# A chunk attention and phase mixer: half of the phase weight on GpSimd's load queue, the first q and k in head halves

## The chip, the cores and the metric

The kernel runs on one core of one Trainium2 chip. The metric is the device time of one execution in microseconds (us). The engines of the core are TensorE (PE; its weight loads are shown as PEld), VectorE (DVE), ScalarE (ACT), GpSimd (POOL) and SyncE (SP); 16 DMA engines move data between HBM and on-chip memory. Engines run their own instruction streams in order and wait for each other through semaphores.

## The reference

Two stages, all inputs fp32. q, k and v are (8 batches, 8 heads, 576 tokens, 64). The first stage is attention inside chunks of 64 tokens; the second, with d_model = 512, mixes phases, tokens and channels.

```python
scores = scale * q_c @ k_c.T            # per batch, head and chunk of 64
attn = exp(scores - max) / sum
x = concat_heads(attn @ v_c)            # (8, 576, 512)

theta = x @ w_theta                     # phase weight, 512 x 512
zr, zi = x * cos(theta), x * sin(theta)
y = w_tok_r @ zr + w_tok_i @ zi         # along tokens, 576 x 576
u = x + y
out = u + max(u @ w_ch, 0)              # 512 x 512
```

## The kernel before

**Tiles.** Batches go in four pairs, p = 0 to 3. The 2 x 576 tokens of a pair are nine tiles of 128, in five groups: A and B are two tiles each of the pair's first batch, C and D two each of its second, and M is the middle tile, which has the last 64 tokens of both batches. A step is named by what it does, an optional part, the pair and the group: `L1.0A` is part 1 of step L for pair 0, group A. Part 0 and part 1 of an attention step are heads 0 to 3 and heads 4 to 7; of a later step they are the two tiles.

**The steps of a group.** `q`, `k`, `v` load it; `L`, `N` or `T` (`qk_t`, L276) transpose q and k on TensorE into PSUM; `tq` and `tkA`/`tkV` (L319) copy them out on VectorE or ScalarE; `S` is the score product (L358), `e` the exponential on ScalarE (L368, L374), `V` the product with v (L392), `n` the division (L404, L406). `X` or `Q` transposes x, `xA`/`xV` copies it (L453), `H` is x @ w_theta (`project`, L470), `g` the cosine and sine on ScalarE (L484, L488), `z` their products with x (L500 to L508). `Y` mixes the tokens (L542, L556), `y` adds x (L582), `U` or `R` transposes u, `W` is u @ w_ch (L470), `w` the ReLU and sum (L590), `s`/`sA` the store. `lw` loads a block of token weights (L227) and `TW` transposes it (L258). `D.n.b` are n products of a zero tile into bank b, which keep TensorE busy and have no other use (L269). `pe` and `pg` switch ScalarE's function table (L137).

**The order** is written out by hand: `ORDER` (L16) is a list of steps, walked once (L661), so every engine's instructions stand in the order of that list. The last numbers of a step are the PSUM banks it uses (8 banks; two steps that use one bank wait for each other's readers).

**Queues.** All loads that cast fp32 to fp16 on the way are issued by POOL: q and k (L180, L188, L193), v (L207, L217), token weights (L227) and w_ch (L243). The program gives POOL's loads eight completion semaphores in turn, and a load waits until the one eight before it has landed. `gate` (L164) also makes the loads of later pairs wait for a division of earlier work. The phase weight is different: `lt` (L229) has SP load it as two fp32 halves of 512 KB into tiles of the pool that q and k use too, and ScalarE (`ct0`) and VectorE (`ct1`) cast them (L240).

**The start.** POOL loads q.0B, builds the identity that the transposes need (`make_identity`, called in `init`, L131), and loads k.0B, then 0M, 0A and the v of 0B, 0A and 0M. TensorE runs 24 dummies, transposes 0B and 0M, runs 7 more dummies, and goes on with 0A.

Of the kernel before, what the change touches and what calls it, by code (L numbers as in the profile page):

```python
# [24 lines left out]
z0.0A z1.0A YA.0A.2 v.0D qP.1B kP.1B L.0D.0.1 tq.1A tkA.0D S.1A.4 V0.0C.6 y.0A e.1A q.1C tq.0D
YA.0B.2 n0.0C V1.0C.0 n1.0C V0.1A.4 V1.1A.6 n1.1A n0.1A YB.0B.2 lw.04 lc.00 q.1M X.0C.0 xV.0C
YM.0B.2 y.0B S.0D.6 Q.1A.4 xV.1A H.0C.0 e.0D V1.0D.2 n1.0D pg.00 g.0C V0.0D.6 H.1A.4 R.0B.2
n0.0D Q.0D.6 xV.0D g.1A k.1M q.1D TW.04.0 k.1D z.0C U.0A.1 H.0D.6 N.1B.4.5 uA.0B uV.0A tq.1B
g.0D z.0D tkA.1B k.1C W.0A.2 v.1C YC.0D.6 v.1B w.0A v.1D N.1M.1 tkV.1M T.1D.4 v.1M S.1B.2 pe.00
e.1B tq.1D tkA.1D tq.1M z.1A YM.0D.6 qP.2A sA.0A YD.0D.6 S.1M.2 twA.04 e.1M L.1C.5.4 tq.1C  # L30
Y.0M.0 y.0D tkA.1C S.1D.2 V1.1B.4 e.1D W.0B.6 V0.1D.2 kP.2A n1.1B S.1C.4 e.1C y.0M w.0B v.2A
YD.0C.0 q.2C q.2B k.2B n0.1D V0.1M.7 V0.1B.2 V1.1D.4 n0.1M V1.1M.6 YC.0C.0 n1.1M X.1M.6 n0.1B
n1.1D xA.1M U.0D.7 YM.0C.0 X.1B.2 v.3M y.0C sA.0B xV.1B q.2M k.2M X.1D.6 v.3D uA.0D N.2A.5.4
tkA.2A U.0C.7 xA.1D W.0D.0 tq.2A v.2B S.2A.2 e.2A R.0M.4 uV.0C uA.0M W.0C.6 V1.1C.2 V0.1C.4 w.0D
w.0C v.2M H.1M.0 pg.00 g.1M n1.1C n0.1C qP.2D W.0M.1 w.0M H.1B.6 V0.2A.4 Q.1C.0 q.3B H.1D.2 g.1B
n0.2A g.1D xV.1C v.3C H.1C.0 k.2C V1.2A.6 z.1M g.1C q.3C T.2B.4 k.3B z.1B tq.2B Y.1A.2 n1.2A
z.1D z.1C y.1A Q.2A.6 tkA.2B S.2B.0 v.2D Y.1D.4 pe.00 e.2B xA.2A V1.2B.6 y.1D V0.2B.0 n0.2B
n1.2B Y.1C.2 X.2B.0 T.2C.4 xV.2B T.2M.6 tq.2C Y.1B.0 tkV.2M tkA.2C S.2C.4 tq.2M S.2M.6 e.2C s.0D
y.1C k.3C kP.2D e.2M q.3A H.2A.2 g.2A y.1B R.1B.0 V0.2M.7 uV.1B v.3A v.2C V1.2M.6 n1.2M N.2D.4.5
n0.2M H.2B.0 g.2B X.2M.6 tkV.2D U.1A.5 v.3B uA.1A xV.2M tq.2D W.1B.2 H.2M.0 g.2M V1.2C.6 z.2A  # L40
# [6 lines left out]
R.2B.4 Q.3D.6 uA.1M e.3M xV.3D uA.2B W.1M.0 S.3C.2 V0.3A.6 y.2M w.1M H.3D.4 e.3C pg.00 g.3D
V1.3A.0 n0.3A n1.3A V1.3C.6 n1.3C W.2B.2 V0.3M.0 V1.3M.1 n1.3M n0.3M Q.3A.6 Y.2D.4 xV.3A R.2A.0
uA.2A w.2B V0.3C.6 y.2D H.3A.2 g.3A R.2C.0 n0.3C Q.3C.6 xV.3C W.2A.4 uV.2C z.3A X.3M.0 s.1C w.2A
H.3C.6 z.3D xA.3M H.3M.0 sA.1M g.3M z.3M W.2C.4 Y.3B.0 g.3C z.3C Y0.3D.2 w.2C y.3B R.2M.0 sA.2B  # L50
R.2D.6 s.2A R.3B.4 Y.3M.3 uA.2D W.2D.6 y.3M U.3M.3 uA.3B Y1.3D.4 y0.3D w.2D y1.3D W.3B.6 w.3B
s.2C s.3B uA.2M W.2M.0 w.2M uA.3M sA.2D Y.3A.2 y.3A Y1.3C.0 R.3A.6 uV.3A R1.3D.2 y1.3C s.2M
# [7 lines left out]
def kernel(  # L60
# [103 lines left out]
    def gate(p):  # L164

        if p and marks:
            nc.gpsimd.tensor_copy(out=seen, in_=marks.pop())
            marks.clear()

    def load_qk(p, g, which, plain):  # L170
        j0, bb, s0 = GROUPS[g]
# [12 lines left out]
        if plain:
            t = t.rearrange("p (j h d) -> p j h d", j=2, h=H)
            for j in range(2):
                t0 = s0 + j * P
# [39 lines left out]
            nc.gpsimd.dma_start(t[0:rows, ri], ap[i * P : i * P + rows, :])  # L227
# [382 lines left out]
    work = {  # L610
        "q": lambda p, g: load_qk(p, g, 0, False),
        "k": lambda p, g: load_qk(p, g, 1, False),
        "qP": lambda p, g: load_qk(p, g, 0, True),
        "kP": lambda p, g: load_qk(p, g, 1, True),
        "v": load_v,
        "lt": lambda p, g: load_theta(),
        "ct0": lambda p, g: cast_theta(0),
        "ct1": lambda p, g: cast_theta(1),
        "lc": lambda p, g: load_w_ch(),
        "lw": lambda p, i: load_tok(i),  # L620
        "init": lambda p, g: setup(),
        "pe": lambda p, g: table(AF.Exp),
        "pg": lambda p, g: table(AF.Sin),
# [80 lines left out]
```

## Time and profile before

| what | value |
|---|---|
| device time, median of 3 runs | 209.05 us (208.4 to 209.28) |
| the profiled execution | 206.72 us, of which its span 205.0 us |
| granted TensorE clock, mean of the span | 0.989 |
| busy: PE | 194.5 us (95%), 3467 products |
| busy: DVE, ACT, POOL | 130.2, 108.3, 94.7 us |
| q0, POOL's queue | 87568 packets, 16.01 MB |
| q1, SP's queue | 3472 packets, 6.42 MB |

The span runs from the first to the last instruction, and what lies around it, 1.72 us here, is start and end of the program. A busy share is an average over stages with different limits: the DMA engines are busy all through the first half and hardly in the last quarter, so the table alone does not say what bounds which stage. A load's time in the DMA view goes from its issue to the landing of its last part; with several loads in flight it is mostly time behind other loads.

### The profile page before, as it was taken

To read this page: it belongs to the slowest core of one execution; us is meant where nothing else is said; L and a number is where in the kernel's file an instruction comes from. 1 tells how busy PE (TensorE), PEld (TensorE's weight loads), DVE (VectorE), ACT (ScalarE), POOL (GpSimd) and SP (SyncE) were. 2 spreads that over 40 slices of the span, in tenths; PEclk is the share of its full clock that TensorE was granted. 3 is DMA by queue.
4 is the path that set the end of the run, shared out by engine and by line. 5 is a ranking of instruction groups with operands and counts; after the bars stand their busy time and mean duration, and the time that the engine had idled before them with its cause. 6 is when DMAs were issued, how large, how long until landed. Compare 5 with 4: busy or idle time off the path is not lost.

```text
span 205.0 us, 7674 instructions
## 1 busy us (share of the span) xinstructions
PE 194.5 (95%) x3467; PEld 103.6 (51%) x3467; DVE 130.2 (64%) x232; ACT 108.3 (53%) x133; POOL 94.7 (46%) x139
## 2 busy tenths in 40 slices
PE   7878999899969999999999999999999999999992
PEld 2355665556536575445546455555554544544441
DVE  0035875597655877893665888379767598253662
ACT  4044989339845168693038961489875345410211
POOL 7788894896977885986593460100000000000000
PEclk9979999999999999999999999999999999999998
DMA  6999999999999999999999995722020034224054
GB/s 211 157 166 126 176 188 170 123 137 163 164 176 191 117 204 222 217 148 161 79 160 82 130 152 36 102 106 106 3 106 3 3 92 168 106 101 155 3 184 176
DMA packets 93312, 26.99 MB, mean 132 GB/s; under 512 B 86368, under 2 KB 88288, under 8 KB 93280
## 3 DMA queue, kind: packets, MB, share of 16 engines
q0 software_dynamic: 87568, 16.01, 97.3%
q1 hardware_dynamic: 3472, 6.42, 8.8%
q10 hardware_dynamic: 2240, 4.06, 5.8%
q8 instruction: 27, 0.44, 0.9%
q14 instruction: 5, 0.04, 0.1%
HBM read 33.06 MB, written 9.44 MB: 207 GB/s over the span
## 4 chain that ended last, share of the span: by engine, by line
PE 78%; DMA 15%; POOL 3%; issue 2%; DVE 0%; ACT 0%; POOLq 0%; ACTq 0%; DVEq 0%
PE ps L556 29%; PE ps L470 29%; DMA v<-in_v_dram 8%; DMA qk<-in_q_dram 7%; PE ps L542 4%; PE ps L439 3%; PE ps L392 3%; PE ps L430 3%; PE ps L358 2%; PE ps L310 2%; PE ps L293 2%; POOL qk L193 1%; POOL wnat L227 1%; POOL v L217 1%; PE ps L297 0%
## 5 line engine op out<-in xcount | busy, mean ns | idle before, releaser
L556 PE MATMUL ps<-zi,wT 128*128 128x512 f16 x144 | 42.7, 379 | 1.8 <-issue 1.8
L556 PEld LDWEIGHTS <-wT 128*128 128x128 f16 x288 | 26.8, 98 | 32.4 <-issue 2.1
L556 PE MATMUL ps<-zr,wT 128*128 128x512 f16 x144 | 42.1, 380 | 0.0
L217 POOL DMA_DIRECT2D v<-in_v_dram x48 | 36.3, 777 | 10.2 <-DMA qk<-in_q_dram 3.7
L582 DVE TENSOR_TENSOR x<-ps,x 128x1024 f16<-128x1024 f32 (+1 forms) x22 | 22.5, 1026 | 22.6 <-PE ps L556 18.2
L470 PE MATMUL ps<-wch,uT 128*128 128x512 f16 (+1 forms) x148 | 34.3, 374 | 0.7 <-ACT uT L453 0.7
L470 PE MATMUL ps<-wtheta,xT 128*128 128x512 f16 x144 | 34.3, 380 | 0.0
L590 DVE SCALAR_TENSOR_TENSOR o<-ps,x 128x1024 f32<-128x1024 f32 (+2 forms) x23 | 22.6, 988 | 8.4 <-PE ps L470 6.5
L453 ACT COPY uT<-ps 128x1024 f16<-128x1024 f16 (+1 forms) x16 | 12.6, 800 | 28.8 <-PE ps L439 24.8
L374 ACT ACTIVATE eT<-ps 128x1024 f16<-128x1024 f32 (+1 forms) x18 | 16.6, 929 | 18.8 <-PE ps L358 18.8
L330 ACT COPY kT<-ps 128x1024 f16<-128x1024 f16 (+1 forms) x15 | 13.3, 901 | 24.9 <-DVE qT L326 13.4
L406 DVE TENSOR_TENSOR x<-ps,recip 128x512 f16<-128x512 f32 (+1 forms) x40 | 25.5, 638 | 1.4
L484 ACT ACTIVATE cos<-ps,pihalf 128x1024 f16<-128x1024 f32 (+1 forms) x22 | 21.1, 957 | 7.0 <-PE ps L470 6.7
L326 DVE COPY qT<-ps 128x1024 f16<-128x1024 f16 (+2 forms) x23 | 12.9, 570 | 17.5 <-PE ps L297 13.0
L470 PEld LDWEIGHTS <-uT 128*128 128x128 f16 x148 | 13.3, 98 | 15.1 <-ACT uT L453 1.9
L470 PEld LDWEIGHTS <-xT 128*128 128x128 f16 x144 | 12.9, 98 | 13.5
L488 ACT ACTIVATE sin<-ps 128x1024 f16<-128x1024 f32 (+1 forms) x22 | 19.0, 863 | 0.0
L193 POOL DMA_DIRECT2D qk<-in_q_dram x13 | 11.9, 920 | 1.4 <-POOLq L688 0.8
L404 DVE RECIPROCAL recip<-ps 128x8 f32<-128x8 f32 (+1 forms) x40 | 7.8, 195 | 7.4 <-PE ps L392 7.3
L453 DVE COPY xT<-ps 128x1024 f16<-128x1024 f16 (+1 forms) x13 | 8.1, 624 | 6.7 <-PE ps L439 4.0
L269 PE MATMUL ps<-zeros 128*128 128x512 f16 x33 | 11.0, 501 | 1.3 <-DVE pihalf L130 1.2
L193 POOL DMA_DIRECT2D qk<-in_k_dram x13 | 11.8, 913 | 0.7 <-issue 0.6
(59 smaller groups left out, 232.1 us busy)
## 6 DMA issues: line engine op xcount, KB each, us to landing
out_dram<-o SPq DMA_DIRECT2D x8, 512.0 KB, 3.4
qk<-in_q_dram POOLq DMA_DIRECT2D x13, 256.0 KB, 6.1
qk<-in_k_dram POOLq DMA_DIRECT2D x13, 256.0 KB, 7.0
out_dram<-o ACTq DMA_DIRECT2D x6, 512.0 KB, 4.1
v<-in_v_dram POOLq DMA_DIRECT2D x40, 64.0 KB, 5.8
v<-in_v_dram POOLq DMA_DIRECT2D x16, 128.0 KB, 6.1
wraw<-in_moe_w_theta_dram SPq DMA_DIRECT2D x2, 512.0 KB, 3.8
qk<-in_q_dram POOLq DMA_DIRECT2D x6, 128.0 KB, 4.9
```

The costliest lines, as they stand in the source:

```text
L193: nc.gpsimd.dma_start(t.rearrange("p (h x) -> p h x", h=H), ap[2 * p + bb, :, s0 : s0 + GT, :].rearrange("h (p s) d -> p h (s d)", s=2),)
L217: nc.gpsimd.dma_start(v16[rows, slot + tile, :, 0:D], v[2 * p + bb, :, t0 : t0 + m, :].rearrange("h s d -> s h d"),)
L330: nc.scalar.copy(out=t.rearrange("p x s c -> p x (s c)").rearrange("p x (c s) -> p x c s", s=2), in_=ps.rearrange("p x s c -> p x c s"),)
L374: nc.scalar.activation(out=eT.rearrange("p h r e c -> p (h r e) c"), in_=ps, func=AF.Exp, scale=scale)
L406: nc.vector.tensor_tensor(out=tokens(p, g, "x")[:, :, f * NE * D : (f + 1) * NE * D].rearrange("p c (h d) -> p c h d", h=NE), in0=psv[:, 0 ...
L453: (nc.vector.tensor_copy if how == "V" else nc.scalar.copy)(out=to.rearrange("p b (r c) -> p b r c", c=CH), in_=psv)
L470: nc.tensor.matmul(ps[:, a * DM : a * DM + cols.stop - cols.start], xT[:, b0 + a, db, :], weight[:, db, cols], start=(db == 0), stop=(db = ...
L484: nc.scalar.activation(out=cos[:, 0:n].rearrange("p a e -> p (a e)"), in_=pin, func=AF.Sin, bias=pihalf, scale=1.0,)
L488: nc.scalar.activation(out=sin[:, 0:n].rearrange("p a e -> p (a e)"), in_=pin, func=AF.Sin)
L556: nc.tensor.matmul(ps[:, a * DM : a * DM + DM], wT[:, kt, t0 : t0 + P], zs[bb], start=(done + k == 0), stop=(done + k == NK - 1),)
L582: nc.vector.tensor_tensor(out=u, in0=ps, in1=u, op=ALU.add)
L590: nc.vector.scalar_tensor_tensor(out=o, in0=ps[:, 0 : n * m].rearrange("p (j d) -> p j d", j=n), scalar=0.0, in1=u, op0=ALU.max, op1=ALU.add,)
```

## The change

Four edits, and new numbers in the order around them:

1. The phase weight's first half stays on SP's queue (`lt0`) and is cast on ScalarE (`ctA`). Its second half is one load on POOL's queue that casts on the way (`lt1`), issued behind k.0A and ahead of v.0B. VectorE's cast goes, and one tile of the pool less is taken.
2. q and k of 0B and of 0A are loaded in head halves: four transfers per group where there were two.
3. The identity is built behind the four issues of 0B (`id`) instead of between q.0B's and k.0B's.
4. Dummies and banks: 24 dummies before L1.0B become 19, D.4 is added before V0.0B, D.2 before V1.0A is dropped, D.2 comes before L.0C and D.3 before TW.02 (33 become 35). `pe` is called before e.0C. Most steps up to the early part of pair 2 use other PSUM banks, by the same pairs of neighbours, and a few later ones do. The steps keep their order otherwise.

```diff
 ORDER = """
-q.0B init.00 k.0B D.20.0 q.0M lt.00 ct0.00 D.4.0 L1.0B.0.1 L0.0B.2.3 tq1.0B tkA1.0B S1.0B.0 k.0M
-tq0.0B tkA0.0B L0.0M.2 tq0.0M L1.0M.3 e1.0B S0.0B.4 q.0A k.0A D.7.0 L1.0A.0.1 tkV0.0M e0.0B v.0B
-tkV1.0M ct1.00 tq1.0A L0.0A.2.4 tkA1.0A S1.0A.0 tkA0.0A tq1.0M v.0A tq0.0A V0.0B.6 n0.0B S0.0A.2
-e1.0A V1.0B.4 D.2.0 V1.0A.0 S0.0M.6 e0.0A v.0M n1.0B n1.0A e0.0M X0.0B.2 xA0.0B X1.0B.3 V0.0A.4
...
+q0.0B q1.0B init.00 k0.0B k1.0B id.00 D.12.0 q.0M lt0.00 ctA.00 D.7.0 L1.0B.0.1 L0.0B.2.3 tq1.0B
+tkA1.0B S1.0B.0 k.0M tq0.0B tkA0.0B L0.0M.2 tq0.0M L1.0M.3 e1.0B S0.0B.4 q0.0A q1.0A k0.0A k1.0A
+D.7.0 L1.0A.0.1 tkV0.0M e0.0B lt1.00 v.0B tkV1.0M tq1.0A L0.0A.2.4 tkA1.0A S1.0A.0 tkA0.0A
+tq1.0M v.0A tq0.0A D.4.2 V0.0B.2 n0.0B S0.0A.6 e1.0A V1.0B.0 V1.0A.2 S0.0M.4 e0.0A v.0M n1.0B
+n1.0A e0.0M X0.0B.0 xA0.0B X1.0B.7 V0.0A.4 lw.01 n0.0A V0.0M.6 S1.0M.2 n0.0M e1.0M H0.0B.0
...
-TW.03.4 twV.03 H0.0A.1 z1.0B H.0M.0 TW.00.2 twV.00 k.0C L.0C.7.6 lw.02 q.1A tq.0C k.1A g.0M z.0M
-g0.0A TW.02.4 YB.0A.2 tkA.0C twA.02 q.0D k.0D S.0C.0 e.0C L.1A.7.6 tkA.1A v.0C v.1A YM.0A.2
...
+twV.01 z0.0B xA.0M lw.00 H1.0A.1 g1.0A TW.03.4 twV.03 H0.0A.0 z1.0B H.0M.7 TW.00.2 twV.00 k.0C
+D.2.1 L.0C.1.6 lw.02 q.1A tq.0C k.1A g.0M z.0M g0.0A D.3.4 TW.02.4 YB.0A.0 tkA.0C twA.02 q.0D
+k.0D S.0C.2 pe.00 e.0C L.1A.7.6 tkA.1A v.0C v.1A YM.0A.0 z0.0A z1.0A YA.0A.0 v.0D qP.1B kP.1B
...
-z.2B z.2M q.3M k.3M W.1A.6 V0.2D.0 n0.2D R.1D.4 Y.2B.2 w.1A T.3D.0 uA.1D y.2B tq.3D V1.2D.6
-n1.2D tkA.3D Y.2A.4 y.2A S.3D.0 sA.0M e.3D Q.2D.6 xA.2D k.3A W.1D.2 w.1D S.3B.0 e.3B V0.2C.6
...
+z.2B z.2M q.3M k.3M W.1A.6 V0.2D.0 n0.2D R.1D.4 Y.2B.2 w.1A T.3D.0 uA.1D y.2B tq.3D V1.2D.6
+n1.2D tkA.3D Y.2A.2 y.2A S.3D.0 sA.0M e.3D Q.2D.6 xA.2D k.3A W.1D.4 w.1D S.3B.0 e.3B V0.2C.6
...
     def setup():
...
-        make_identity(nc, id16)
...
-    def load_qk(p, g, which, plain):
+    def load_qk(p, g, which, plain, f=None):
...
-        ap = (q, k)[which]
+        hs = slice(0, H) if f is None else slice(f * NE, f * NE + NE)
+        ap = (q, k)[which][:, hs]
...
         nc.gpsimd.dma_start(
-            t.rearrange("p (h x) -> p h x", h=H),
+            t.rearrange("p (h x) -> p h x", h=H)[:, hs],
...
     def load_theta():
-        for a in range(2):
-            t = nat.tile([P, 2, DM], FP32, name="wraw", tag="nat")
-            wraw.append(t)
-            nc.sync.dma_start(
-                t,
-                moe_w_theta[a * GT : a * GT + GT, :].rearrange("(a p) e -> p a e", p=P),
-            )
-
-    def cast_theta(a):
-        copy = nc.vector.tensor_copy if a else nc.scalar.copy
-        copy(out=wtheta16[:, 2 * a : 2 * a + 2], in_=wraw[a])
+        t = nat.tile([P, 2, DM], FP32, name="wraw", tag="nat")
+        wraw.append(t)
+        nc.sync.dma_start(t, moe_w_theta[0:GT, :].rearrange("(a p) e -> p a e", p=P))
+
+    def cast_theta(copy):
+        copy(out=wtheta16[:, 0:2], in_=wraw[0])
+
+    def load_theta_rest():
+        nc.gpsimd.dma_start(
+            wtheta16[:, 2:4], moe_w_theta[GT:DM, :].rearrange("(a p) e -> p a e", p=P)
+        )
...
+        "id": lambda p, g: make_identity(nc, id16),
```

More of the change, by code (lines that the diff above doesn't have):

```diff
@@ L16 @@
 ORDER = """
-q.0B init.00 k.0B D.20.0 q.0M lt.00 ct0.00 D.4.0 L1.0B.0.1 L0.0B.2.3 tq1.0B tkA1.0B S1.0B.0 k.0M
-tq0.0B tkA0.0B L0.0M.2 tq0.0M L1.0M.3 e1.0B S0.0B.4 q.0A k.0A D.7.0 L1.0A.0.1 tkV0.0M e0.0B v.0B
-tkV1.0M ct1.00 tq1.0A L0.0A.2.4 tkA1.0A S1.0A.0 tkA0.0A tq1.0M v.0A tq0.0A V0.0B.6 n0.0B S0.0A.2
-e1.0A V1.0B.4 D.2.0 V1.0A.0 S0.0M.6 e0.0A v.0M n1.0B n1.0A e0.0M X0.0B.2 xA0.0B X1.0B.3 V0.0A.4
-lw.01 n0.0A V0.0M.7 S1.0M.0 n0.0M e1.0M H0.0B.2 Q1.0A.0 Q0.0A.4 V1.0M.6 xA1.0B xV0.0A g0.0B
-H1.0B.3 n1.0M TW.01.4 lw.03 xV1.0A g1.0B q.0C X.0M.0 twV.01 z0.0B xA.0M lw.00 H1.0A.7 g1.0A
@@ L23 @@
-TW.03.4 twV.03 H0.0A.1 z1.0B H.0M.0 TW.00.2 twV.00 k.0C L.0C.7.6 lw.02 q.1A tq.0C k.1A g.0M z.0M
-g0.0A TW.02.4 YB.0A.2 tkA.0C twA.02 q.0D k.0D S.0C.0 e.0C L.1A.7.6 tkA.1A v.0C v.1A YM.0A.2
[L25 to L40, printed above, removed]
@@ L41 @@
-w.1B n1.2C R.1C.4 Y.1M.1 s.0C s.1B S.2D.2 uV.1C y.1M q.3D k.3D T.3B.4 tq.3B pe.00 e.2D tkA.3B
-z.2B z.2M q.3M k.3M W.1A.6 V0.2D.0 n0.2D R.1D.4 Y.2B.2 w.1A T.3D.0 uA.1D y.2B tq.3D V1.2D.6
-n1.2D tkA.3D Y.2A.4 y.2A S.3D.0 sA.0M e.3D Q.2D.6 xA.2D k.3A W.1D.2 w.1D S.3B.0 e.3B V0.2C.6
-H.2D.4 n0.2C V0.3B.0 n0.3B V1.3B.6 pg.00 g.2D sA.1A W.1C.2 Q.2C.0 n1.3B T.3C.6 tkA.3C xV.2C
-X.3B.4 H.2C.0 w.1C tq.3C xA.3B z.2D N.3M.2 g.2C tq.3M H.3B.6 g.3B tkV.3M z.2C T.3A.4 V1.3D.0
-tq.3A z.3B Y.2C.2 n1.3D U.1M.0 tkA.3A S.3A.4 pe.00 e.3A y.2C V0.3D.6 n0.3D Y.2M.1 sA.1D S.3M.2
@@ L47 @@
[L47 to L52, printed above, removed]
@@ L53 @@
-R0.3D.4 uA0.3D W.3M.1 uA1.3D W0.3D.7 W1.3D.0 U1.3C.2 w.3M w1.3D W.3A.4 w0.3D Y0.3C.3 uA1.3C s.3M
-W1.3C.0 w.3A y0.3C s0.3D s1.3D R0.3C.6 s.3A uA0.3C w1.3C sA1.3C W2.3C.0 w2.3C sA2.3C W3.3C.7
-w3.3C s3.3C
+q0.0B q1.0B init.00 k0.0B k1.0B id.00 D.12.0 q.0M lt0.00 ctA.00 D.7.0 L1.0B.0.1 L0.0B.2.3 tq1.0B
+tkA1.0B S1.0B.0 k.0M tq0.0B tkA0.0B L0.0M.2 tq0.0M L1.0M.3 e1.0B S0.0B.4 q0.0A q1.0A k0.0A k1.0A
+D.7.0 L1.0A.0.1 tkV0.0M e0.0B lt1.00 v.0B tkV1.0M tq1.0A L0.0A.2.4 tkA1.0A S1.0A.0 tkA0.0A
+tq1.0M v.0A tq0.0A D.4.2 V0.0B.2 n0.0B S0.0A.6 e1.0A V1.0B.0 V1.0A.2 S0.0M.4 e0.0A v.0M n1.0B
@@ new lines @@
+n1.0A e0.0M X0.0B.0 xA0.0B X1.0B.7 V0.0A.4 lw.01 n0.0A V0.0M.6 S1.0M.2 n0.0M e1.0M H0.0B.0
+Q1.0A.2 Q0.0A.4 V1.0M.1 xA1.0B xV0.0A g0.0B H1.0B.7 n1.0M TW.01.4 lw.03 xV1.0A g1.0B q.0C X.0M.3
+twV.01 z0.0B xA.0M lw.00 H1.0A.1 g1.0A TW.03.4 twV.03 H0.0A.0 z1.0B H.0M.7 TW.00.2 twV.00 k.0C
+D.2.1 L.0C.1.6 lw.02 q.1A tq.0C k.1A g.0M z.0M g0.0A D.3.4 TW.02.4 YB.0A.0 tkA.0C twA.02 q.0D
+k.0D S.0C.2 pe.00 e.0C L.1A.7.6 tkA.1A v.0C v.1A YM.0A.0 z0.0A z1.0A YA.0A.0 v.0D qP.1B kP.1B
+L.0D.2.3 tq.1A tkA.0D S.1A.6 V0.0C.4 y.0A e.1A q.1C tq.0D YA.0B.0 n0.0C V1.0C.2 n1.0C V0.1A.6
@@ new lines @@
+V1.1A.4 n1.1A n0.1A YB.0B.0 lw.04 lc.00 q.1M X.0C.2 xV.0C YM.0B.0 y.0B S.0D.4 Q.1A.6 xV.1A
+H.0C.2 e.0D V1.0D.0 n1.0D pg.00 g.0C V0.0D.6 H.1A.4 R.0B.0 n0.0D Q.0D.2 xV.0D g.1A k.1M q.1D
+TW.04.7 k.1D z.0C U.0A.6 H.0D.2 N.1B.4.5 uA.0B uV.0A tq.1B g.0D z.0D tkA.1B k.1C W.0A.0 v.1C
+YC.0D.2 v.1B w.0A v.1D N.1M.4 tkV.1M T.1D.0 v.1M S.1B.5 pe.00 e.1B tq.1D tkA.1D tq.1M z.1A
+YM.0D.2 qP.2A sA.0A YD.0D.2 S.1M.4 twA.04 e.1M L.1C.0.1 tq.1C Y.0M.7 y.0D tkA.1C S.1D.0 V1.1B.2
+e.1D W.0B.4 V0.1D.0 kP.2A n1.1B S.1C.2 e.1C y.0M w.0B v.2A YD.0C.6 q.2C q.2B k.2B n0.1D V0.1M.5
@@ new lines @@
+V0.1B.0 V1.1D.2 n0.1M V1.1M.4 YC.0C.6 n1.1M X.1M.4 n0.1B n1.1D xA.1M U.0D.5 YM.0C.6 X.1B.0 v.3M
+y.0C sA.0B xV.1B q.2M k.2M X.1D.4 v.3D uA.0D N.2A.3.2 tkA.2A U.0C.5 xA.1D W.0D.6 tq.2A v.2B
+S.2A.0 e.2A R.0M.2 uV.0C uA.0M W.0C.4 V1.1C.0 V0.1C.2 w.0D w.0C v.2M H.1M.7 pg.00 g.1M n1.1C
+n0.1C qP.2D W.0M.6 w.0M H.1B.4 V0.2A.0 Q.1C.2 q.3B H.1D.6 g.1B n0.2A g.1D xV.1C v.3C H.1C.0 k.2C
+V1.2A.2 z.1M g.1C q.3C T.2B.4 k.3B z.1B tq.2B Y.1A.6 n1.2A z.1D z.1C y.1A Q.2A.0 tkA.2B S.2B.2
+v.2D Y.1D.4 pe.00 e.2B xA.2A V1.2B.6 y.1D V0.2B.0 n0.2B n1.2B Y.1C.2 X.2B.0 T.2C.4 xV.2B T.2M.6
@@ new lines @@
+tq.2C Y.1B.0 tkV.2M tkA.2C S.2C.4 tq.2M S.2M.6 e.2C s.0D y.1C k.3C kP.2D e.2M q.3A H.2A.2 g.2A
+y.1B R.1B.0 V0.2M.7 uV.1B v.3A v.2C V1.2M.6 n1.2M N.2D.4.5 n0.2M H.2B.0 g.2B X.2M.6 tkV.2D
+U.1A.5 v.3B uA.1A xV.2M tq.2D W.1B.2 H.2M.0 g.2M V1.2C.6 z.2A w.1B n1.2C R.1C.4 Y.1M.1 s.0C s.1B
+S.2D.2 uV.1C y.1M q.3D k.3D T.3B.4 tq.3B pe.00 e.2D tkA.3B z.2B z.2M q.3M k.3M W.1A.6 V0.2D.0
+n0.2D R.1D.4 Y.2B.2 w.1A T.3D.0 uA.1D y.2B tq.3D V1.2D.6 n1.2D tkA.3D Y.2A.2 y.2A S.3D.0 sA.0M
+e.3D Q.2D.6 xA.2D k.3A W.1D.4 w.1D S.3B.0 e.3B V0.2C.6 H.2D.2 n0.2C V0.3B.0 n0.3B V1.3B.4 pg.00
@@ new lines @@
+g.2D sA.1A W.1C.6 Q.2C.0 n1.3B T.3C.4 tkA.3C xV.2C X.3B.3 H.2C.0 w.1C tq.3C xA.3B z.2D N.3M.2
+g.2C tq.3M H.3B.6 g.3B tkV.3M z.2C T.3A.4 V1.3D.0 tq.3A z.3B Y.2C.2 n1.3D U.1M.0 tkA.3A S.3A.4
+pe.00 e.3A y.2C V0.3D.6 n0.3D Y.2M.1 sA.1D S.3M.2 R.2B.4 Q.3D.6 uA.1M e.3M xV.3D uA.2B W.1M.0
+S.3C.2 V0.3A.6 y.2M w.1M H.3D.4 e.3C pg.00 g.3D V1.3A.0 n0.3A n1.3A V1.3C.6 n1.3C W.2B.2 V0.3M.0
+V1.3M.1 n1.3M n0.3M Q.3A.6 Y.2D.4 xV.3A R.2A.0 uA.2A w.2B V0.3C.6 y.2D H.3A.2 g.3A R.2C.0 n0.3C
+Q.3C.6 xV.3C W.2A.4 uV.2C z.3A X.3M.0 s.1C w.2A H.3C.6 z.3D xA.3M H.3M.0 sA.1M g.3M z.3M W.2C.4
@@ L56 @@
+Y.3B.0 g.3C z.3C Y0.3D.2 w.2C y.3B R.2M.0 sA.2B R.2D.6 s.2A R.3B.4 Y.3M.3 uA.2D W.2D.6 y.3M
+U.3M.3 uA.3B Y1.3D.4 y0.3D w.2D y1.3D W.3B.6 w.3B s.2C s.3B uA.2M W.2M.0 w.2M uA.3M sA.2D Y.3A.2
+y.3A Y1.3C.0 R.3A.6 uV.3A R1.3D.2 y1.3C s.2M R0.3D.4 uA0.3D W.3M.1 uA1.3D W0.3D.7 W1.3D.0
+U1.3C.2 w.3M w1.3D W.3A.4 w0.3D Y0.3C.3 uA1.3C s.3M W1.3C.0 w.3A y0.3C s0.3D s1.3D R0.3C.6 s.3A
+uA0.3C w1.3C sA1.3C W2.3C.0 w2.3C sA2.3C W3.3C.7 w3.3C s3.3C
 """.split()
@@ L188, in load_qk @@
                 nc.gpsimd.dma_start(
-                    t[:, j], ap[2 * p + bb, :, t0 : t0 + P, :].rearrange("h s d -> s h d")
+                    t[:, j, hs],
+                    ap[2 * p + bb, :, t0 : t0 + P, :].rearrange("h s d -> s h d"),
                 )
@@ L610 @@
     work = {
[L611 to L614, printed above, removed]
         "v": load_v,
-        "lt": lambda p, g: load_theta(),
-        "ct0": lambda p, g: cast_theta(0),
-        "ct1": lambda p, g: cast_theta(1),
+        "lt0": lambda p, g: load_theta(),
+        "lt1": lambda p, g: load_theta_rest(),
+        "ctA": lambda p, g: cast_theta(nc.scalar.copy),
+        "ctV": lambda p, g: cast_theta(nc.vector.tensor_copy),
+        "id": lambda p, g: make_identity(nc, id16),
         "lc": lambda p, g: load_w_ch(),
@@ L630 @@
     parted = {
+        "q": lambda p, g, f: load_qk(p, g, 0, False, f),
+        "k": lambda p, g, f: load_qk(p, g, 1, False, f),
+        "qP": lambda p, g, f: load_qk(p, g, 0, True, f),
+        "kP": lambda p, g, f: load_qk(p, g, 1, True, f),
         "T": lambda p, g, f, *banks: qk_t(p, g, f, "small", *banks),
```

## The prediction

> **What bounds the kernel now.** I read four views, from coarse to fine: the page's 40 slices, the chain of waits, the timeline around the places where the chain changes engine, and busy time by stretch. First the slices (one digit is 5.1 us):
>
> ```profile
> PE   7878999899969999999999999999999999999992
> ...
> PEclk9979999999999999999999999999999999999998
> DMA  6999999999999999999999995722020034224054
> ```
>
> The 16 DMA engines are full from the second slice to the 24th, and the tensor engine from the fifth to the last. Both look like the bound for the first 40 us, so the chain of waits decides (start, length, what):
>
> ```profile
> 1.24 8.14 DMA qk<-in_q_dram
> 9.39 0.28 issue
> 9.67 6.77 DMA v<-in_v_dram
> 16.44 0.28 issue
> 16.73 2.13 POOL wnat L227 x4
> 18.85 6.12 DMA qk<-in_q_dram
> ...
> 28.97 9.26 DMA v<-in_v_dram
> 38.22 0.04 issue
> 38.26 0.29 PE ps L392 x13
> ```
>
> Up to 38.26 us the chain is loads on GpSimd's queue; from there it is tensor work to the end, one stall of 1.80 us at 58.6 apart. The last load in it, one of batch 1's v for group 0C, lands at 38.22. The tensor engine's own rows show how far it is from being the bound there:
>
> ```profile
> 37.27 0.53 PE L392 MATMUL ps<-v,eT 64*64 64x65 f16 x3
> 38.26 0.29 PE L392 MATMUL ps<-v,eT 64*64 64x65 f16 x13 [0.46 <-DMA v<-in_v_dram]
> ```
>
> V0.0C begins at 37.27, does 3 of its 16 products and stands until 38.26. So the tensor engine is early by 0.9 us at most. Whatever the change wins ahead of this point, the end moves only by what this landing moves, and by 0.9 us at most if the landing alone moves.
>
> **The change, part by part.**
>
> *Half of the phase weight leaves SyncE's queue.* Its two transfers (512 KB each) are issued at 0.74 and 1.23 and take 3.4 and 4.2 us, so they land at 4.1 and 5.4: the second keeps the DMA engines 1.3 us. In that stretch the load queue moves almost nothing (200 packets of 0.05 MB between 1.8 and 5.3 us). Without it the loads of 0B, 0M and 0A should land 1.3 us earlier. The price comes behind k.0A, ahead of v.0B: 512 KB read on the load queue. Not in the trace in this form. From below, the 1.3 us of SyncE's own transfer; from above, half of w_ch, which is read in the same shape with the same cast and lands at 51.9, 3.5 us after the load before it: 1.75. Nearest in bytes is a q or k load, also 512 KB read with a cast: k.1A lands at 33.1 and q.0D at 34.6, 1.45 apart. I take 1.5. For everything behind it the sum is 1.5 − 1.3 = +0.2 us, from 0 to +0.45; and down to −0.3, because the DMA share falls to 1.37 between 16 and 20 us (2.23 before, 2.04 after 28), so some of the added transfer may fit there. The cast on VectorE (0.68 us at 13.88) goes; VectorE was idle around it, so that is worth nothing.
>
> *Halves.* POOL issues four transfers where it issued two, for 0B and for 0A. A whole one costs 0.92 us of POOL (L193), one of half the rows 0.69 (L180), so 2 × 0.9 us more. The identity (0.54 us from 2.25 to 2.79) moves behind the four issues of 0B; its first reader is a transpose at 8 us or later, so that costs nothing. POOL reaches v.0B at 1.24 + 8 × 0.69 + 0.54 + 4 × 0.69 + 0.6 (the weight, as L227's 0.58) = 10.7 us, against 9.67. Queued behind it are the other v, then the token weights at 16.73. Every load waits for the one eight before it to land (the ninth, v.0B, goes 0.28 us after q.0B landed), and the token weights' first issue is released by v.0B landing at 16.44, which becomes 16.6. POOL itself is there by 10.7 + 6.1 (eight issues of v) = 16.8, so the two tie and I cost the issues at nothing; if the tie breaks the wrong way, they cost up to 1.0 us.
>
> Smaller transfers are also where the Trainium skill speaks against the change: "DMA: Bandwidth & Descriptors", section "Anatomy of one DMA — SWDGE (gpsimd) path", gives each transfer a fixed 2.0 us or so. Paid in line, five more would be an estimated 10 us. The trace disagrees for a queue that is kept full: the four small loads of 0M land at 11.2, 11.7, 12.1 and 12.6, 0.45 us apart.
>
> *Dummies.* 24 dummy products before the first transposes become 19, at 0.43 us until 5.8 and 0.215 after: done at 7.7 instead of 8.8, before q.0B's new landing at 8.1. Four new ones stand ahead of V0.0B, which must wait for v.0B (now 17.2, then 17.4; it begins at 18.00 now); two before V1.0A go. V0.0B and V1.0A gain 0.6 and 0.3 us by their loads. The first transposes of 0B then give up to 0.45 of it back: in the new bank numbering they wait for the second norm of 0B (20.16), where the first two began at 19.71. Then D.2 before L.0C and D.3 before TW.02 add 5 × 0.215 = 1.07 us with no wait to hide in, except 0.3 us at L.1A (its k lands at 33.1). So V0.0C begins at 37.27 + 1.07 − 0.3, less 0 to 0.3: at 37.7 to 38.05, still ahead of its load at 38.4. Hidden, with 0.4 us to spare. The extra table switch (pe before e.0C) only adds its 0.20 us activation to ScalarE.
>
> *Banks.* Most steps up to pair 2 get other PSUM banks. I compared, in both programs, the latest instruction that each tensor step waits for, and put the old times beside it. Behind 38 us only one new wait has no slack: Y.2A takes banks 2 and 3, which Y.2B has just left, instead of 4 and 5, so it waits for y.2B on VectorE (L582).
>
> ```profile
> 125.22 0.71 PE L310 MATMUL ps<-id,qk 64*64 64x64 f16 x64
> 125.40 1.23 DVE L582 TENSOR_TENSOR x<-ps,x 128x1024 f16<-128x1024 f32 x1 [0.72 <-PE ps L556]
> 125.75 0.32 PE L392 MATMUL ps<-v,eT 64*64 64x65 f16 x16
> 126.00 0.60 PE L556 MATMUL ps<-zr,wT 128*128 128x512 f16 x2
> ```
>
> Y.2A starts at 126.00 and its banks would be free at 126.63: +0.6 us. Queued behind it is the whole tensor stream, which is busy without a hole for the next 70 us, so all of it reaches the end. The bound from below is nothing (if Y.2A comes late for another reason), from above 0.7.
>
> *Sum.* +0.2 (landing of v.0C) + 0.6 (Y.2A) = +0.8 us. The profiled execution took 206.72 us, of which its span is 205.0; it becomes 207.5. The runs shown are slower (median 209.05); I add the difference there: **209.9 us**, +0.4%. A measurement here can tell about 0.5% (1.05 us) from no change, so this is "no change" leaning to slower.
>
> **The rivals.**
>
> *The lead carries through (faster).* If the added half slips into the thin stretch at 16 to 20 us and all loads stay 1.3 us early, V0.0C no longer waits. But it gains no more than 0.9 − (1.07 − 0.3) + 0.3, some 0.4 us, with the dummies on the path; without them showing, 0.9. With Y.2A's 0.6 the end is −0.3 to +0.2: 208.75 to 209.25. For it: the first loads do start late. Against it: the DMA row has no hole behind the fifth slice.
>
> *The clock (slower).* The tensor engine's stretches (length, PE busy, PEld, DVE, ACT, POOL, clock, DMA):
>
> ```profile
> 8.85:12.64 3.79, 1.83 (x52) 1.30 (x52) 0.85 (x2) 1.34 (x3) 2.43 (x4) 1.00 1.95 170
> 12.64:16.06 3.42, 3.35 (x34) 1.78 (x35) 1.38 (x4) 0.87 (x2) 3.20 (x5) 0.50 2.23 149
> ```
>
> After 3.8 us of half-idle waiting the granted clock is 0.50 for 3.4 us. With loads earlier and fewer dummies the waits move to 14 to 19 us; if the half-speed stretch falls on 16 to 19.5, it doubles about 1.7 us of real work there. V0.0C then begins at 39.4 to 39.75 instead of 38.4: +1.0 to +1.35 on top of 0.8, 210.9 to 211.2. It decides once V0.0C begins later than 38.4, that is from 0.4 us of lost time on. The Trainium skill ("TensorE: Matmul & The Clock Gate", "HAM oscillation") asks only for no gap above some 3.4 us; by it this rival could not happen. The trace differs: the longest idle of the tensor engine there is 1.0 us, and the clock fell, so I keep the rival.
>
> *POOL's issues decide (slower).* v.0B and all behind it 1.0 us later: 210.9.
>
> *The stall at 58.6 (either way).* It has no cause in the trace; gone, it would give 208.1, doubled, 211.7.
>
> **How the numbers follow.** Forecast 0.47; lead carries through 0.15; clock 0.14; POOL 0.12; stall 0.12, halved between its ends. The range should leave out 2 in 10: it reaches from 208.4 (the lead, with the landing term at its −0.3) to 211.5 (the clock, with that term at +0.45), and leaves out the ends of the stall and of mixtures. The forecast alone, by its terms, spans 209.0 to 210.2. Faster by over 0.5% (below 208.0) needs the stall gone, or more than the lead can give: 0.07. Slower (above 210.1): clock, POOL, half of the stall and the top of the forecast, 0.38. Within: 0.55.
>
> **What would show it.** q.0B's second half landing at 8.1 and k.0A's at 14.1 (15.4 now) would show the early lead right; v.0C's last landing within 0.5 us of 38.2 and a longer wait, or none, of V0.0C on it, the conserved bytes; an idle of 0.6 us at Y.2A, ended by VectorE's L582, the bank; a clock of 0.50 behind 16.1, the clock rival; POOL busy without a hole until 17 and v.0B landing past 17.5, POOL's. I am wrong if v.0C lands over 0.5 us off, or if tensor work between 38 and 126 changes by more than 0.5 us.

## The result, and the profile after

The changed kernel takes 208.94 us (median of 12 runs, 207.43 to 215.34) against 206.76 us for the kernel before (12 runs): a ratio of 1.0111, 95% interval [1.0068, 1.0154], some 2.3 us slower. The time lies inside the range of the prediction, but the change is larger than forecast: +1.1% instead of +0.4%. The three runs that the prediction started from (median 209.05) were the three longest of these twelve; that lifted the forecast time, not the forecast difference. Put on the twelve runs, the range would reach from 206.1 to 209.2, and the measured time would lie near its upper end.

Some executions of every kernel are slower than its others; ratios leave them out, and since the first profile of the changed kernel was such a one (as were the only ones of `bank_alone` and `weight_filled` below, which are read by their ratios), the profile shown is its second. It is the run `after_again`, of 208.10 us with a span of 206.3 us (ratio 1.0124 [1.0084, 1.0164]). Its slices:

```profile
PE   7665999999999999999999998999999999999992
...
PEclk9999699999999999999999999999999999999999
DMA  5999999999999999999999995722020034224063
```

The tensor engine is less busy in slices 2 to 4 (665 instead of 878), and the clock falls in the fifth slice instead of the third. Before, that fell mostly on waiting and dummies; now it falls on real work. The chain of waits up to V0.0C (start, length, what):

```profile
2.87 1.51 POOL qk L194 x2
...
4.95 2.70 POOL qk L180 x4
7.65 3.01 POOL qk L194 x4
10.66 0.69 POOL wtheta L239
11.35 1.49 POOL v L218 x2
12.84 6.41 DMA v<-in_v_dram
...
23.16 1.66 PE ps L471 x4
...
25.33 0.97 PE ps L471 x4
...
31.20 0.54 PE ps L270 x2
...
32.75 0.75 PE ps L270 x3
...
40.63 0.38 PE ps L359 x32
41.00 0.13 PE ps L393 x14
```

Before, this stretch was a chain of transfers. Now it is POOL's issuing up to 12.84, the transfer of the third and last part of v.0B, and then tensor work without a wait for any load. The added dummies (L270) stand in it with 0.54 and 0.75 us, and one group of four x @ w_theta products takes 1.66 us where the next takes 0.97: that is the half clock. POOL's own rows (start, length, what; the bracket is idle time and what ended it):

```profile
1.24 1.65 POOL L194 DMA_DIRECT2D qk<-in_q_dram  x2 [0.80 <-POOLq L691]
...
7.60 1.58 POOL L194 DMA_DIRECT2D qk<-in_q_dram  x2
9.11 1.55 POOL L194 DMA_DIRECT2D qk<-in_k_dram  x2
10.57 0.79 POOL L239 DMA_DIRECT2D wtheta<-in_moe_w_theta_dram  x1
11.26 4.62 POOL L218 DMA_DIRECT2D v<-in_v_dram  x6
...
18.44 0.56 POOL L228 DMA_DIRECT2D wnat<-in_moe_w_tok_r_dram  x1 [0.40 <-DMA v<-in_v_dram]
```

POOL issues without a hole from 1.24 to 16.6. A half takes 0.79 us (the four pairs: 1.65, 1.51, 1.58 and 1.55). v.0B is first issued at 11.26 (9.67 before), its last part lands at 19.25 (17.19), and the token weights start at 18.44 (16.73). V0.0C on the tensor engine:

```profile
39.54 1.08 PE L298 MATMUL ps<-id,qk 128*64 128x128 f16 x32
40.56 0.45 PE L359 MATMUL ps<-qT,kT 64*64 64x64 f16 x32
40.83 0.30 PE L393 MATMUL ps<-v,eT 64*64 64x65 f16 x16
```

All 16 products go in one piece at 40.83, with no wait: v.0C landed at 40.10, so the load is 1.9 us late (38.22 before) and the tensor engine later still. At Y.2A, which before began at 126.00 without a wait:

```profile
126.06 1.23 DVE L583 TENSOR_TENSOR x<-ps,x 128x1024 f16<-128x1024 f32 x1 [0.72 <-PE ps L557]
...
127.34 0.59 PE L557 MATMUL ps<-zr,wT 128*128 128x512 f16 x2 [0.55 <-DVE x L583]
```

The new wait is there, 0.55 us idle, ended by y.2B. And behind it all, the stall is gone. In the profile of before (first fence) one product stands from 58.21 to 60.39; in that of the changed kernel (second) the same stretch runs through:

```profile
58.21 0.38 PE L556 MATMUL ps<-zi,wT 128*128 128x512 f16 x1
60.39 0.38 PE L556 MATMUL ps<-zi,wT 128*128 128x512 f16 x1 [1.80 <-issue]
```

```profile
59.97 0.60 PE L557 MATMUL ps<-zi,wT 128*128 128x512 f16 x2
60.41 0.59 PE L557 MATMUL ps<-zr,wT 128*128 128x512 f16 x2
60.84 0.59 PE L557 MATMUL ps<-zi,wT 128*128 128x512 f16 x2
```

Where the time went between the two profiles, at the start of the same products: V0.0C's last products +2.57 us (38.26 to 40.83); the stall −1.96 (2.18 start to start against 0.22); Y.2A +0.66 (from the 2001st to the 2501st product that is no dummy, 19.60 to 20.26). The sum, +1.27, comes close to the difference of the spans, 1.36 us (204.95 to 206.32). The runs say +2.3, so this one execution does not show the whole loss; the experiments come back to that.

### The profile page after: what moved, and what is told of

The parts are those of the page before. It is cut to its first block, busy times and chain, and to the rows that moved or that the text cites. A ratio compares the mean times of both kernels' runs of the same rounds, so it can differ in the third digit from the quotient of the medians.

```text
span 209.0 us, 7678 instructions
## 1 busy us (share of the span) xinstructions
PE 195.9 (94%) x3469; PEld 104.4 (50%) x3469; DVE 129.7 (62%) x231; ACT 108.7 (52%) x134; POOL 97.9 (47%) x144
## 4 chain that ended last, share of the span: by engine, by line
PE 87%; POOL 4%; DMA 3%; issue 2%; DVE 1%; ACT 1%; DVEq 0%; ACTq 0%; POOLq 0%
PE ps L471 31%; PE ps L557 31%; PE ps L543 4%; PE ps L440 3%; PE ps L431 3%; PE ps L393 3%; PE ps L359 3%; DMA qk<-in_k_dram 3%; POOL qk L194 2%; PE ps L298 2%; PE ps L311 2%; PE ps L294 2%; PE ps L270 1%; PE ps L259 1%; POOL qk L180 1%
## 5 line engine op out<-in xcount | busy, mean ns | idle before, releaser
L194 POOL DMA_DIRECT2D qk<-in_q_dram x15 | 13.1, 879 | 2.0 <-POOLq L691 0.8
L194 POOL DMA_DIRECT2D qk<-in_k_dram x15 | 13.0, 876 | 0.8 <-issue 0.8
L270 PE MATMUL ps<-zeros 128*128 128x512 f16 x35 | 12.1, 506 | 1.2 <-DVE pihalf L130 1.2
```

Of the source, the lines that this page charges most:

```text
L194: nc.gpsimd.dma_start(t.rearrange("p (h x) -> p h x", h=H)[:, hs], ap[2 * p + bb, :, s0 : s0 + GT, :].rearrange("h (p s) d -> p h (s d)", ...
L270: nc.tensor.matmul(psum(bank, 1), zeros[:, 0:P], zeros)
```

## The experiments

Three theories stood against each other: POOL's **issues** of halves delay every load behind them; the **clock** falls on real work; the **order** (dummies and banks) costs by itself. A fourth, that the half weight on the load queue costs, was the prediction's first term. Ratios are to the kernel before, run beside each kernel. Times in the table are of one profile each: when the last part of v.0B landed, when the clock was at 0.50 in the first 30 us, when the last products of V0.0C began, and how long the tensor engine then stood in the stall between 57 and 62 us.

| run | ratio [95%] | v.0B | clock 0.50 | V0.0C | stall |
|---|---|---|---|---|---|
| before | 1 | 17.19 | 12.64–16.06 | 38.26 | 1.80 |
| after_again | 1.0124 [1.0084, 1.0164] | 19.25 | 21.12–24.53 | 40.83 | none |
| whole_loads | 1.0137 [1.0085, 1.0188] | 17.44 | 16.64–23.46 | 39.36 | 2.17 |
| weight_on_sp | 1.0106 [1.0055, 1.0157] | 17.39 | none | 38.82 | 1.21 |
| tail_banks | 1.0135 [1.0088, 1.0181] | 18.77 | 15.46–18.88, 22.29–25.70 | 40.83 | none |
| loads_alone | 1.0108 [1.0064, 1.0152] | 19.14 | 15.51–25.75 | 40.59 | 0.49 |
| weight_and_identity | 1.0057 [1.0017, 1.0096] | 17.19 | 17.15–20.56 | 37.49 | 1.40 |
| no_added_dummies | 1.0142 [1.0096, 1.0188] | 19.19 | 15.41–25.65 | 40.62 | none |
| order_alone | 1.0121 [1.0025, 1.0218] | 17.41 | none | 38.12 | 2.51 |
| loads_filled | 1.0121 [1.0032, 1.0210] | 19.99 | none | 40.20 | none |
| late_front | 1.0047 [1.0002, 1.0092] | 17.59 | 11.13–14.54 | 40.32 | none |

**One part of the change undone.** The changed kernel again, and three kernels that each take one part back:

```diff
 # whole_loads
-q0.0B q1.0B init.00 k0.0B k1.0B id.00
+q.0B init.00 k.0B id.00
-q0.0A q1.0A k0.0A k1.0A
+q.0A k.0A
 # weight_on_sp
-lt1.00 v.0B tkV1.0M
+v.0B tkV1.0M ct1.00
 # tail_banks (with six later steps renumbered as in the kernel before)
-Y.2A.2
+Y.2A.4
```

> The changed kernel as it is, for a second profile and as the measure of the others. Issue theory (GpSimd's four extra transfers starve the load queue): GpSimd issues without a hole of over 0.4 us from 1.2 to past 15 us, each half costs about 0.8 us of it instead of the 0.69 that was forecast, and the DMA share between 8.9 and 12.6 us is well below before's 1.95. Weight theory (the half on the load queue costs more than its 1.5 us): the weight's landing lies over 1.7 us behind k.0A's second half. Clock theory: the granted clock is 0.50 somewhere behind 16 us. All: 1.0 to 1.2% slower than the kernel before, and 0.6 us idle at Y.2A.

> The changed kernel with q and k of 0B and 0A loaded whole again (four issues fewer), all else as changed. Issue theory: v.0B's first landing comes 1.5 us or more earlier than in the changed kernel, and 1 to 1.5 us of its 2.3 us loss are regained. Weight theory and clock theory: less than 0.5 us regained, v.0B lands as late.

> The changed kernel with both halves of the phase weight on SyncE's queue again and VectorE's cast back in its place; halves, identity, dummies and banks as changed. Weight theory: 1 us or more regained, because the load queue has 1.5 us less to move behind k.0A. Issue theory: the first loads are 1.3 us later, GpSimd has one issue less (0.8 us), v.0B lands about 0.5 us earlier at most, and less than 0.5 us is regained or some is lost.

> The changed kernel with the PSUM banks of Y.2A and of the six later steps that differ as they were before (Y.2A on banks 4 and 5). All theories: the idle of 0.6 us ahead of Y.2A goes and the time falls by 0.6 us; if the tensor stream were not the bound there, nothing changes.

No ratio falls by what its theory promised, and with intervals of some 1 us to each side a part worth less would not show. In `after_again` itself the signs of all three theories came: POOL without a hole, a clock of 0.50 behind 16 us, and the weight 2.12 us behind k.0A's second half (14.96 and 17.08), where 1.7 was the sign. In the other profiles with this load it is 0.71 to 1.80 us, so that is one execution's.

Whole loads bring v.0B back to 17.44, as the issue theory said, but the clock is at 0.50 for 6.8 us and V0.0C begins 1.1 us late, now by the tensor engine; and the stall is back. With the weight back on SyncE's queue v.0B lands at 17.39, 1.86 us earlier where the issue theory had allowed 0.5, though its third part is issued at 12.96, no earlier than in the changed kernel (12.84). There the clock does not fall, v.0C lands at 38.54 and V0.0C begins only 0.56 us late; still the ratio is 1.0106, so the 1 us or more that the weight theory promised is not regained either. In its profile a stall of 1.21 us takes most of the gain: 2.0 us ahead of the changed kernel at V0.0C, it is 0.28 ahead at the 1001st product (62.89 against 63.17). With the old banks the wait at Y.2A is gone from the trace (from the 2001st to the 2501st product: 19.59 us, as before), but an interval of some 1 us to each side cannot show 0.66 us.

**The other way round: one part alone in the kernel before**, and the added dummies taken out of the changed kernel:

```diff
 # bank_alone
-Y.2A.4
+Y.2A.2
 # weight_and_identity: half of the weight on POOL's queue, identity behind
-lt.00 ct0.00
+lt0.00 ctA.00
-e0.0B v.0B tkV1.0M ct1.00
+e0.0B lt1.00 v.0B tkV1.0M
-q.0B init.00 k.0B
+q.0B init.00 k.0B id.00
 # loads_alone: as weight_and_identity, and q and k of 0B and 0A in halves
 # no_added_dummies, in the changed kernel
-D.4.2 V0.0B.2
+V0.0B.2
-D.2.1 L.0C.1.6
+L.0C.1.6
-D.3.4 TW.02.4
+TW.02.4
```

> The kernel before with one edit: Y.2A takes banks 2 and 3 instead of 4 and 5. The tail-bank theory: this edit alone costs the 0.66 us that its wait took out of the profile of the changed kernel (19.60 to 20.26 us between the 2000th and the 2500th product), a ratio of 1.003 to the kernel before. Rival (the wait is hidden once the kernel is otherwise that of before): ratio 1.000. Up to Y.2A at 126 us the two programs are the same, so whatever differs in the first 126 us of the profiles (the clock, the stall at 58.6, the first landings) is the variation from execution to execution of the kernel before.

> The kernel before with its own dummies and banks, and all three edits of the loads: half of the phase weight on POOL's queue, q and k of 0B and 0A in head halves, identity behind the four issues. Issue theory (POOL's issues of halves and what they do to the landing of v.0B decide): v.0B lands behind 18.5 as in the changed kernel (19.25) and the time is 1 us or more over the kernel before, ratio about 1.007. Dummy theory (the 5 products added before L.0C and TW.02 put TensorE behind the loads): without them V0.0C waits for its load again and the ratio is at most 1.003. Clock theory: the ratio goes by where the half-speed stretch lies, 3.4 us of it behind 16 us costing about 1.7 us.

> The kernel before with its own dummies, banks and whole loads of q and k; half of the phase weight on POOL's queue and the identity behind the issues of 0B. Issue theory: without halves v.0B lands by 17.5 and nothing is lost up to 38 us: ratio 0.998 to 1.002. Weight theory (the half on the load queue itself delays v.0C): v.0C lands 0.5 us or more later than before's 38.2 and the ratio is 1.003 or more. Dummy theory: ratio at most 1.002 too, so this run parts weight from the other two.

> The changed kernel without the dummies that it adds: D.4 before V0.0B, D.2 before L.0C and D.3 before TW.02. Dummy theory: the 5 later ones are 1.07 us of TensorE's path, which was the later of the two at V0.0C (TensorE there at 40.65, v.0C landed at 40.10): about 0.5 to 1.0 us come back, ratio 1.007 to 1.010. Issue theory: V0.0C then waits for the load, which lands late all the same: at most 0.5 us come back, ratio 1.010 or more. Clock theory: with fewer dummies TensorE is idle longer and the clock falls to half for longer: no gain, or a loss.

`bank_alone` has a ratio of 1.0055 [1.0022, 1.0088], 0.5 to 1.8 us: the 0.66 us of the wait lies in it, no cost at all does not. `loads_alone` against `weight_and_identity` differs in the halves only: v.0B lands at 19.14 instead of 17.19, V0.0C begins at 40.59 instead of 37.49, and the excess doubles (the intervals still overlap; the landings are what settles it). So with the half weight on POOL's queue it is the halves that delay the loads. But it takes both: v.0B lands at 17.19 (before) and 17.41 (`order_alone`, below) with neither, at 17.39 with halves alone (`weight_on_sp`), at 17.19 and 17.44 with the half weight alone (`weight_and_identity`, `whole_loads`), and at 18.77 to 19.99 with both. Two profiles of one program differ by some 0.4 us here (17.19 before, 17.59 in `late_front`, below). Taking the dummies out gives nothing, against the dummy theory: the clock falls for longer, and V0.0C then waits for its load:

```profile
40.12 0.29 PE L391 MATMUL ps<-v,eT 64*64 64x65 f16 x3
40.62 0.29 PE L391 MATMUL ps<-v,eT 64*64 64x65 f16 x13 [0.21 <-DMA v<-in_v_dram]
```

**Order alone, and the waits filled.** The order of the changed kernel with the loads of before, and the two kernels above with dummies where the tensor engine waited:

```diff
 # loads_filled, in loads_alone
-D.7.0 L1.0A.0.1
+D.18.0 L1.0A.0.1
-V0.0B.6
+D.6.6 V0.0B.6
 # weight_filled, in weight_and_identity
-V0.0B.6
+D.8.6 V0.0B.6
```

> The loads of the kernel before (both weight halves on SyncE's queue, whole q and k, identity in the old place) under the order of the changed kernel: its dummies, banks and table switch. Order theory (dummies and banks cost by themselves): TensorE reaches V0.0C at 37.27 + 1.07 (five dummies) + 0 to 0.45 (first transposes of 0B) = 38.3 to 38.8 against its load at 38.2, so 0.1 to 0.5 us there, and Y.2A's 0.66 behind it: 0.8 to 1.2 us, ratio 1.004 to 1.006. Coverage theory (the dummies are hidden, as the prediction had it): Y.2A's 0.66 alone, ratio 1.003. Load theory (all of the loss comes from the loads): 1.000 to 1.003.

> The three edits of the loads in the order of before, as in the run with the loads alone (ratio 1.0108, half-speed stretch of 10.2 us behind a hole of 2.97 us in L1.0A), with the hole filled: 18 dummies instead of 7 before L1.0A and 6 more before V0.0B, where TensorE stood waiting for loads. Clock theory: the half-speed stretch goes or becomes short, the mean clock rises from 0.980 to 0.988 or more, and 1 to 2 us come back: ratio 1.001 to 1.005. Issue theory: v.0B still lands at 19.1 and v.0C at about 40.5, V0.0C waits for it whatever the clock: ratio 1.008 or more.

> Half of the weight on POOL's queue, whole q and k, identity behind the issues, order and banks of before, as in the run with weight and identity (ratio 1.0057, v.0C at 37.45, half-speed stretch of 3.4 us from 17.15 behind a wait of 2.3 us for v.0B), with 8 dummies in that wait, before V0.0B. Clock theory: the half-speed stretch goes, mean clock from 0.983 to 0.990, about 1 us comes back, ratio 0.997 to 1.002, and it is the best of these kernels. Weight theory: the load queue is what costs, nothing comes back: ratio 1.005 or more.

`loads_filled` parts clock from issues. Its stretches (length, PE busy, PEld, DVE, ACT, POOL, clock, DMA) and its V0.0C:

```profile
15.50:20.00 4.50, 2.69 (x55) 1.62 (x54) 1.04 (x3) 1.61 (x3) 2.12 (x4) 1.00 2.02 136
20.00:25.70 5.70, 5.34 (x164) 3.06 (x163) 4.68 (x13) 3.65 (x6) 5.46 (x10) 1.00 1.24 142
```

```profile
39.56 0.48 PE L390 MATMUL ps<-v,eT 64*64 64x65 f16 x3
40.20 0.29 PE L390 MATMUL ps<-v,eT 64*64 64x65 f16 x13 [0.17 <-DMA v<-in_v_dram]
```

The clock is 1.00 there, and 0.996 to 1.000 in the mean over each of the runs compared (0.975 to 0.983 in `loads_alone`), as the clock theory wanted, and yet V0.0C stands for its load until 40.16: up to here the late loads hold the place by themselves, whatever the clock. Over the runs the ratio, 1.0121, is not below that of `loads_alone`, but the interval from 1.0032 still touches the 1.001 to 1.005 that the clock theory promised, so the time alone does not exclude it.

`order_alone` is too wide to weigh (1.0025 to 1.0218), but its profile is plain: V0.0C begins at 38.12, so in it the added dummies are covered when the loads are those of before, and the 701st product comes at 46.08 (46.17 before). What this execution loses, it loses in a stall of 2.51 us with 3.4 us of half clock behind it, and at Y.2A. `weight_filled` is open: 1.0047 [0.9980, 1.0114] can neither confirm nor exclude that filling that wait pays.

**Is a delay carried to the end?** The table shows a pattern: where V0.0C begins by 39.4, the stall is 1.2 to 2.5 us; where it begins behind 40, 0.5 or none. (The changed kernel's first profile breaks it, with 2.72 us and V0.0C at 40.58.) `late_front` tests it, with tensor work delayed and nothing else changed:

```diff
-V0.0C.6
+D.14.6 V0.0C.6
```

> The kernel before with 14 dummies (3.0 us at 0.215) put ahead of V0.0C, which begins at 37.27 and stands for its load until 38.26 there: 0.99 us of them are covered, so all tensor work behind it begins about 2.0 us later, as late as in the changed kernel, while the loads, the first 37 us and Y.2A's banks stay those of before. Absorption theory (the stall at 58.2, in which 1985 of TensorE's instructions had run when a packet of instructions arrived, is a time set by the DMA queue and not by TensorE, so a late TensorE meets a short stall or none): the product that stands 2.18 us in the profile of before stands less than 1.2, tensor work behind 62 us is 0 to 0.8 us later, ratio 1.000 to 1.004. Rival (a delay ahead of 40 us is carried to the end in full): the stall stays at about 2 us and the ratio is 1.009 to 1.011.

Its tensor rows at V0.0C and where the stall was:

```profile
37.20 3.19 PE L267 MATMUL ps<-zeros 128*128 128x512 f16 x14
40.32 0.32 PE L390 MATMUL ps<-v,eT 64*64 64x65 f16 x16
```

```profile
59.42 0.60 PE L554 MATMUL ps<-zi,wT 128*128 128x512 f16 x2
59.86 0.59 PE L554 MATMUL ps<-zr,wT 128*128 128x512 f16 x2
60.29 0.59 PE L554 MATMUL ps<-zi,wT 128*128 128x512 f16 x2
```

V0.0C goes 2.06 us late, the stall is gone, and the 1501st product comes only 0.39 us late (88.33 against 87.94). In the profile the delay is taken back almost whole; over the runs, +1.0 us [0.0, 1.9] of the 2.06 is left, between the two theories and too wide to choose. My reading is that the stall takes back what it happens to be long in that execution.

## Why the prediction was right or wrong

- **The half weight (+0.2 us): sign and size not confirmed, harmless by itself.** In `weight_and_identity` v.0B lands at 17.19, as before, and v.0C at 37.45, 0.77 us earlier (forecast 0.3 earlier to 0.45 later); in `whole_loads`, with the same loads, v.0C comes 0.58 us later (38.80). The first loads gain more than 1.3 us: q.0B's last part lands at 6.79 against 9.39.
- **POOL's issues (costed at nothing): the step that failed.** The prediction kept the early start of the loads as a gain and let two paths to the token weights tie at 16.6 to 16.8. The start came early enough: q.0B's second half lands at 6.81 (the sign was 8.1) and 0M at 10.13, 2.44 us ahead of before. But k.0A lands at 14.96, not at 14.1: of the lead 0.49 us is left, where `whole_loads` keeps 2.75 (12.70). Between 9 and 15 us POOL's queue moves 0.84 MB in the changed kernel and 0.73 to 0.84 in every profile with halves, against 0.97 to 1.04 in every one without: POOL, issuing without a hole, feeds it too slowly. Start to start a half takes 0.76 us, not the 0.69 of L180, so v.0B is first issued at 11.26, not 10.7. Behind k.0A the weight takes 2.12 us and v.0B's parts 0.43 more than before: −0.49 + 2.12 + 0.43 is the 2.06 us by which v.0B lands late, where the rival had 1.0. Both signs named for this rival came: POOL without a hole to 16.6, v.0B past 17.5. v.0C lands 1.9 us late, past the 0.5 us that the prediction gave itself. So issues and early start were not two terms to be added: the halves used up the lead that was to pay for the weight. Why halves alone cost nothing at v.0B (17.39) is not shown; that the queue, with SyncE's second half in front, has enough waiting to cover the slower issuing is my reading.
- **The dummies (hidden, 0.4 us to spare): right with the old loads, not with the new.** `order_alone` hides them. In the changed kernel the tensor engine reaches V0.0C at 40.83, 3.56 us later than before, of which 0.99 was spare. In the trace: +1.06 by the 145th product (v.0B's landing), +1.49 to the 251st, +0.66 to the 344th and +0.35 to the 461st (the dummies, 1.01 against 0.77 forecast).
- **The clock (a rival at 0.14): it happened, in size as worked out, some 5 us further on.** Of the +1.49, some 1.3 us is half speed: the same products take 5.40 us in the changed kernel, 4.10 to 4.14 in three profiles with no half-speed stretch there (`loads_filled`, `order_alone`, `weight_on_sp`), 3.91 before. The rival said +1.0 to +1.35 for a stretch at 16 to 19.5 us; it came at 21.12 to 24.53, so that the size agrees is in part luck.
- **Y.2A (+0.6): right.** 0.66 us in the profile, gone from it with the old banks, and the one edit alone costs 0.5 to 1.8 us in the old kernel.
- **The stall (no cause in the trace): it is not free of the change.** The prediction let it stand. It mostly shrinks as tensor work comes late, so some of the loss ahead of it is given back.

The failed step and the clock work in parallel: in the changed kernel the load is there at 40.10 and the tensor engine at 40.83. So undoing either alone can't return more than the other leaves, and what it does return meets a longer stall.

That V0.0C comes late by the loads, the clock and the dummies is shown; that this is what makes the kernel 2.3 us slower is not. The sizes do add up: a 2 us delay at the front alone leaves +1.0 us [0.0, 1.9] over the runs, the bank wait alone has +1.1 [0.5, 1.8], together 2.1 against 2.3 measured. But `weight_on_sp`, where V0.0C begins 0.56 us late, has 1.0106, and `order_alone`, where it begins on time, has 1.0121 [1.0025, 1.0218]. One profile each puts that on the stall and Y.2A. A rival that no run parts from it is that the new order, by its other bank numbers and dummies, costs time of its own behind V0.0C. Where the rest of the loss arises stays open. None of these kernels is shown to beat the kernel before.

## What to carry to other kernels

Splitting a transfer costs its issuer nearly a whole further issue (0.79 us for a half, 0.92 for a whole, here), and where one engine issues everything, count when it reaches each later load; a tie between issuing and landing is not a zero. Two changes to one queue need not add: here halves alone and the weight alone left v.0B where it was, and both together moved it by 2 us. When two causes end at the same place, undoing one shows nothing: put each alone into the old kernel too, and read where the other takes over. And ask of every early gain or loss whether a stall further on absorbs it before adding it to the end.

## What the runs showed of the hardware

**The stall meets a fetch of instructions.** The page has a DMA queue that the prediction did not read:

```profile
q8 instruction: 27, 0.44, 0.9%
```

Before, its seventh packet (16 KB, as the 0.44 MB over 27) runs from 58.04 to 59.03. By its end 1985 of the tensor engine's instructions (products and weight loads) had begun, 2 more than at its start: the engine stands there. In `order_alone` the packet runs from 58.00 to 58.96, again at 1985, and the engine stands 2.51 us. In the changed kernel it runs from 57.77 to 58.67, when 1777 had begun; in `late_front` from 56.53 to 57.51, with 1791. There the engine runs on. In every profile with a stall of over 1 us exactly 1985 had begun by the packet's end, in every other one fewer (1771 to 1980). So it looks as if the engine stands when it reaches that instruction ahead of the packet. The packet has no fixed time, though: it starts at 54.42 us in `loads_filled` and at 60.65 in `no_added_dummies`. That it is this that the engine waits for is inferred from the times; no run changed the fetch alone, and why the engine goes on 1.4 us after the packet is open.

**Half-speed stretches come in steps**: 3.41, 6.82 and 10.24 us here. In `loads_alone` the tensor engine stood 2.75 us just ahead of one, in `order_alone` 2.51; in the changed kernel the longest idle in the 5 us ahead of 21.12 was 0.82, with one of 1.93 before that. The Trainium skill ("TensorE: Matmul & The Clock Gate", "HAM oscillation") states the rule as no idle gap above some 3.4 us; these clocks fell with shorter gaps. But `loads_filled`, with a longest idle of 1.58 us there and dummies in the rest of its waits, kept 1.00.

**A first load was late by its last part.** With both weight halves on SyncE's queue, q.0B's last part lands 2.65 us behind the middle ones (6.74 and 9.39). With one, in `weight_and_identity`, it is 0.6 us (6.18 and 6.79). The first transfer's last part lags by 2.0 to 2.7 us in all five profiles with both halves there, and by some 1.0 us or less in the nine with one. That would be how the first loads gained more than the bytes alone would give.
